# Small products of constants in TensorE's planned idle time, in the first chunks of an attention and two-MLP kernel

## The chip, the core and the metric

The kernel runs on one core of one Trainium2 chip. Its engines each follow an instruction list of their own: TensorE (PE in the profile, with its weight loads as PEld), VectorE (DVE), ScalarE (ACT), GpSimd (POOL, idle here) and SyncE (SP), which issues every DMA. Engines wait for one another through semaphores. The metric is the device time of one execution in microseconds (us), the median over the runs shown.

## The reference

Sparse attention over 4 batches, 8 heads, 576 positions of 64 elements, then two MLPs on the 2304 tokens of width 512 (512 to 2048 to 512, and a gated one, 512 to 1536 to 512). Half of the heads attend to the last 32 positions, the others to every 32nd one.

In short:

```python
scores = scale * np.matmul(q, k.transpose(0, 1, 3, 2))
masks = [mask_local if h < H // 2 else mask_strided for h in range(H)]
attn = softmax(np.where(masks, scores, -1e9))
x = np.matmul(attn, v)
h = x @ w_in;  x = np.maximum(0.01 * h, h) @ w_out
gate = 1.0 / (1.0 + np.exp(-(x @ w_gate)))
out = (gate * (x @ w_val)) @ w_out2
```

## The kernel before

Attention is cut into 8 chunks of 288 tokens (half a batch each), a chunk into groups: a pair of heads each, of up to five blocks of 64 queries (in some chunks a pair is two groups). For every group TensorE makes the scores (`sc`, line 510), VectorE masks and scales them (line 530), takes the row maximum and later normalizes (line 556), ScalarE takes the exponentials (line 541), TensorE transposes the result (`pt`, line 565), ScalarE copies that out (`pts`, line 571), and TensorE multiplies with the values (`xo`, line 582). ScalarE and VectorE then split `xo` into a high and a low half, `x` (lines 601 and 599).

Between the groups TensorE already works on the first MLP, in steps of 256 tokens. A step makes `h` (12 products of 128x128 weights with 256 columns, lines 330 to 332: high by high, high by low, low by high), ScalarE and VectorE apply the activation and split it into `gh` and `gl`, and TensorE makes `y` from these in the same way. Everything in attention is float32; the MLP products are in the rounded form fp32r. VectorE and ScalarE also split the weights, which arrive as 64-bit words (`raw`, `w`, `u`, lines 134 to 187). The second MLP follows after attention and the first one, and is TensorE work almost alone.

The order of the first part is not written out by hand. A planner (`Plan`) holds each step with a cost in ns, what it must come after and which buffers or PSUM banks it takes and gives back. `order` chooses step after step for each engine, notes a start time for each, and the program emits all steps in the order of these starts. Each engine then runs its list strictly in that order and waits where a semaphore isn't there yet, so the planner's times set the order and never the real time. `Plan.order` takes, for a step of TensorE, the later of three times: when the engine comes free, when the data is there, and when the PSUM bank is given back. The constants (`cst`: the 128x128 identity and the masks) come in three DMAs at the start, of which `plan.const[1]` is the identity.

The score banks are `mm0` to `mm3`, which `h` shares; `pt` and `xo` use `ax0` and `ax1`, in the first chunk `xo` takes `ya` and `yb`.

Of the kernel before, what the change touches and what calls it, by code (L numbers as in the profile page):

```python
# [59 lines left out]
RING = 12  # L60
STAGED = 2
EARLY = 2
WORDS = 4
SPLIT = 2
OPS = 12
# [7 lines left out]
def attention_mlp_glu(ctx: ExitStack, tc: tile.TileContext, qT, kl, ks0, ks1, vl, vs0, vs1, w1, w2, wg, wv, w3, const, out):  # L73
    nc = tc.nc
# [13 lines left out]
    def sums_of(i):  # L88
        if i not in sum_y:
            sum_y[i] = res.tile([P, KC, 2 * TP], F32, tag=f"sum{i}", bufs=1, name=f"sum_y{i}")  # L90
        return sum_y[i]

    turn, mm_order = dict.fromkeys(BANKS, 0), [0, 1, 2, 3]

    def bank(tag, shape, name):
        if tag in BANKS:
            n, turn[tag] = turn[tag], (turn[tag] + 1) % BANKS[tag]
            tag = f"{tag}{mm_order[n] if tag == 'mm' else n}"
        return ps.tile(shape, F32, tag=tag, bufs=1, name=name)
# [185 lines left out]
    for c in range(NC2):  # L285
        quarter = {n: parts_tile(("p", c, n), [P, 2, 512]) for n in range(1, 8)}
        for m, w in enumerate((wg, wv)):
            d = {n: quarter[n][:, m, :] for n in quarter}
            a, b = Job((w, 2 * c)), Job((w, 2 * c + 1))
            a.whole = b.whole = False  # L290
            a.dest, b.dest, b.only = [d[1], d[2]], [None, d[3]], 1
            t = Sums(a, b, None, [d[5], d[6]])
# [45 lines left out]
    ident = cst[:, 0:P]  # L338
# [9 lines left out]
    class Plan:  # L348
# [9 lines left out]
        def __init__(self, room):  # L358
            self.ops, self.const, self.late = [], [], []
            self.room = {k: [0.0] * n for k, n in room.items()}  # L360
            self.lanes, self.bus, self.held = [0.0] * 8, 0.0, {}

        def add(self, eng, cost, run, rank, me=None, kind=None, after=(), take=(), give=(), then=()):
            op = {
# [6 lines left out]
        def lend(self, op, name, n):  # L371

            at = len(self.room[name])
            self.room[name] += [None] * n
            self.held[op["n"], name] = [at + i for i in range(n)]
            op["give"] += [(name, op)] * n

        def free(self, after, me, *rooms):

# [2 lines left out]
        def order(self):  # L382

            free = dict.fromkeys(("PE", "DVE", "ACT", "SP", "-"), 0.0)
            last, todo, out = "mm", list(self.ops), []
            held = self.held
            while todo:
                best = None
                for eng in free:
                    can = []  # L390
                    for op in todo:
                        if op["eng"] != eng or any(a["end"] is None for a in op["after"] + op["then"]):
                            continue
                        t = max([0.0 if eng == "-" else free[eng]] + [a["end"] + 40 for a in op["after"]])
                        for k in set(op["take"]):
                            units = sorted(x for x in self.room[k] if x is not None)
                            n = op["take"].count(k)
                            if len(units) < n:
                                t = None
                                break  # L400
                            t = max(t, units[n - 1])
                        if t is None:
                            continue
                        if eng == "PE":
                            t = max(t, free[eng] + self.GAP.get((last, op["kind"]), 0))
                        can.append((t, op))
                    if can:
                        t0 = min(t for t, _ in can) + self.NEAR[eng]
                        t, op = min((c for c in can if c[0] <= t0), key=lambda c: (c[1]["rank"], c[1]["n"]))
                        if best is None or t < best[0]:  # L410
                            best = (t, op)
                assert best, [(o["eng"], o["rank"], o["kind"]) for o in todo[:20]]
                t, op = best
                eng = op["eng"]
                for k in op["take"]:
                    u = min((x, i) for i, x in enumerate(self.room[k]) if x is not None)[1]
                    self.room[k][u] = None
                    op["at"].setdefault(k, []).append(u)
                    held.setdefault((id(op["me"]), k), []).append((op, u))
                    held.setdefault((op["n"], k), []).append(u)  # L420
                if eng == "SP":
                    lane = min(range(8), key=lambda i: self.lanes[i])
                    t = max(t, self.lanes[lane])
                    free[eng] = t + 450
                    self.bus = max(self.bus, t + 1300) + op["cost"] / (280 if t < 25000 else 330)
                    op["end"] = self.lanes[lane] = self.bus + 900
                else:
                    free[eng] = t + op["cost"]
                    op["end"] = t + op["cost"] + self.TAIL[eng]
                    if eng == "PE":  # L430
                        last = op["kind"]
                for k in op["give"]:
                    if isinstance(k, tuple):
                        k, who = k
                        u = held[who["n"], k].pop(0)
                    else:
                        u = held[id(op["me"]), k].pop(0)[1]
                    self.room[k][u] = op["end"] + 40
                todo.remove(op)
                op["start"] = t  # L440
                out.append(op)
            return sorted(out, key=lambda o: o["start"])

    class Group:
# [52 lines left out]
        def scores(self, at):  # L497
            nb, w, cut = self.nb, self.w, self.cut
            sc = [
                bank(f"mm{j + 2 * ('h' in at)}", [P, z - a, w], f"sc{a}") for j, (a, z) in enumerate(((0, cut), (cut, nb)))  # L500
            ]
            for i in range(cut):
                for n in (i, cut + i):
                    if n >= (cut, nb)[n >= cut]:
                        continue
                    q0, k0 = self.q0[n] - self.q0[0], self.k0[n] - self.k0[0]
                    for h in range(2):
                        r = slice(64 * h, 64 * h + 64)
                        o = self.side(n, h)
                        nc.tensor.matmul(  # L510
                            sc[n >= cut][o, n - cut * (n >= cut), :], self.q[r, q0 : q0 + 64], self.k[r, k0 : k0 + w],
                            start=True, stop=True,
                        )
            self.sc = sc
# [45 lines left out]
        def tr(self, a, z, at):  # L560
            if a == 0:
                self.pt = {}
            self.pt[a] = bank(f"ax{at['ax'][0]}", [P, z - a, P], "pt")
            for n in range(a, z):
                nc.tensor.transpose(self.pt[a][: self.w, n - a, :], self.e[:, n, :], ident)  # L565

# [6 lines left out]
        def pv(self, at):  # L573
            nb, w = self.nb, self.w
            total = sum(self.nq)
            self.xo = bank(f"ax{at['ax'][0]}" if "ax" in at else "ya" if "ya" in at else "yb", [P, total], "xo")
            col = 0
            for n in range(nb):
                for h in range(2):
                    r = slice(64 * h, 64 * h + 64)  # L580
                    a = self.side(n, h).start + self.skip[n]
                    nc.tensor.matmul(
                        self.xo[r, col : col + self.nq[n]], self.v[:w, n, r], self.p[:w, n, a : a + self.nq[n]],
                        start=True, stop=True,
                    )
                col += self.nq[n]
# [88 lines left out]
    class First:  # L675
# [11 lines left out]
        def enter(self, last, at):  # L687
            u = unit(self.u[0])
            self.h = bank(f"mm{(at['h'][0] + 2) % 4}", [P, self.T], "h")
            for k in range(KC):  # L690
                xh, xl = xs(self.t0, self.t1, k)
                products(self.h, u, k * P, (k + 1) * P, xh, xl, k == 0, k == KC - 1)
            if last:
                vacant.append(places[self.u[0]])
# [282 lines left out]

    consts = [(P, P + 2 * LW), (0, P), (P + 2 * LW, CONST_W)]

    def load_const(a, z):  # L980
        nc.sync.dma_start(out=cst[:, a:z], in_=const[:, a:z])

    plan = Plan(
        {
            "place": RING, "qk": 3, "v": 2, "e": 3, "st": 3, "sc": 1, "h": 2, "ax": 2, "ya": 1, "yb": 1, "pts": 2, "early": EARLY, "late": EARLY, "raw": STAGED, "w32": WORDS, "split": 1, "late split": SPLIT, "sums": 2,
        }
    )
    unit_done, unit_place = {}, {}
    for j, (a, z) in enumerate(consts):
        op = plan.add("SP", 4 * P * (z - a), lambda at, a=a, z=z: load_const(a, z), rank=((0.5, 1.5, 2.5)[j],), me=plan)  # L990
# [20 lines left out]
    for j in range(RING, RING + n_a):  # L1011
        op = plan.add(
            "SP", 4096 * P, lambda at, j=j: fetch(j), rank=(-2000 + j,), after=[jobs[ready[uses[j]]].kept], then=before,
            take=["place"], me=plan,
# [41 lines left out]
        began = [op]  # L1056
    with tc.manual_schedule(engines={nc.tensor.engine, nc.vector.engine, nc.scalar.engine, nc.sync.engine}):
        for op in plan.order():
            op["run"](op["at"])
    planning.clear()  # L1060
    load_places()
# [96 lines left out]
```

## Time and profile before

| | |
|---|---|
| median of 3 runs | 917.87 us (916.51 to 923.81) |
| profiled execution: its own time | 922.54 us |
| profiled execution: span from the first to the last instruction | 920.7 us |
| TensorE busy | 900.1 us, 98% |
| VectorE busy | 603.7 us, 66% |
| ScalarE busy | 426.7 us, 46% |

The profiled execution lies within the three runs' spread, 4.67 us above their median. In a row of the profile, a line such as L510 is a line of the kernel, an arrow points from what is read to what is written, `128*63 128x128` is the stationary operand and then the output, and x20 counts the records merged into the row. A float32 product leaves two records. Granted clock 1.00 stands for 2.4 GHz and 0.50 for 1.2 GHz. TensorE's matmuls overlap in their records; how fast they follow on one another is read from their starts.

### The profile page before, as it was taken

How to read it: one execution, taken by the hardware profiler on the slowest of the kernel's cores; microseconds unless marked ns; L12 is line 12 of the kernel's file. 1: busy time of each engine (PE TensorE's matmuls, PEld its weight loads, DVE VectorE, ACT ScalarE, POOL GpSimd, SP SyncE). 2: the span in 40 equal slices, each digit the busy share in tenths (PEclk: the TensorE clock that was granted, in tenths of full speed). 3: DMA queues.
4: the chain of work that ended last, by engine and by line, in shares of the span. 5: the costliest groups of instructions: out<-in, count | busy, mean ns of one | idle time of the engine just before them, and what ended most of it. 6: DMA issues, size and time to landing. Idle time of an engine off the chain costs nothing.

```text
span 920.7 us, 16036 instructions
## 1 busy us (share of the span) xinstructions
PE 900.1 (98%) x5904; PEld 818.6 (89%) x5904; DVE 603.7 (66%) x1285; ACT 426.7 (46%) x1127; POOL 0.2 (0%) x4
## 2 busy tenths in 40 slices
PE   6899999999999999999999999999999999999997
PEld 4778888998888999888899999999999999999996
DVE  6798899856877587786796535567535555535554
ACT  6688788644454344443545442243343232243330
POOL 0000000000000000000000000000000000000000
PEclk9889999999999999999999999999999999999999
DMA  8454846767675579664549766555766556755522
GB/s 239 141 153 123 258 127 205 225 217 294 245 241 196 180 264 377 227 206 155 189 134 376 265 209 207 208 210 203 277 214 211 206 207 208 276 208 208 211 79 69
DMA packets 72030, 194.47 MB, mean 211 GB/s; under 512 B 9144, under 2 KB 20760, under 8 KB 71952
## 3 DMA queue, kind: packets, MB, share of 16 engines
q1 hardware_dynamic: 71952, 193.44, 61.2%
q8 instruction: 47, 0.77, 0.3%
q14 instruction: 31, 0.25, 0.1%
HBM read 149.90 MB, written 43.52 MB: 210 GB/s over the span
## 4 chain that ended last, share of the span: by engine, by line
PE 93%; DMA 3%; ACT 2%; DVE 1%; SPq 1%; issue 0%
PE h L330 8%; PE h L331 7%; PE h L332 7%; PE y L330 7%; PE y L331 7%; PE y L332 7%; PE o L934 5%; PE o L933 5%; PE o L932 5%; PE va L889 3%; PE ga L891 3%; PE ga L889 3%; PE ga L890 3%; PE va L890 3%; PE va L891 3%; PE pt L565 2%
## 5 line engine op out<-in xcount | busy, mean ns | idle before, releaser
L330 PE MATMUL h<-x,u 128*128 128x256 f32 (+2 forms) x384 | 133.1, 347 | 0.0
L330 PE MATMUL y<-gh,u 128*128 128x256 f32 (+2 forms) x384 | 131.1, 341 | 0.0
L331 PE MATMUL h<-x,u 128*128 128x256 f32 (+2 forms) x384 | 130.8, 341 | 0.0
L332 PE MATMUL h<-x,u 128*128 128x256 f32 (+2 forms) x384 | 130.7, 340 | 0.0
L331 PE MATMUL y<-gl,u 128*128 128x256 f32 (+2 forms) x384 | 129.3, 337 | 0.0
L332 PE MATMUL y<-gh,u 128*128 128x256 f32 (+2 forms) x384 | 129.3, 337 | 0.0
L937 DVE TENSOR_TENSOR sum_o<-o,sum_o 128x512 f32<-128x512 f32 x90 | 62.1, 691 | 47.2 <-PE o L934 47.2
L704 ACT ACTIVATE gh<-h 128x256 fp32r<-128x256 f32 (+2 forms) x96 | 47.0, 489 | 80.9 <-PE y L332 74.2
L934 PE MATMUL o<-u,gl 128*128 128x512 f32 x216 | 84.4, 391 | 0.0
L933 PE MATMUL o<-u,gh 128*128 128x512 f32 x216 | 84.3, 390 | 0.0
L932 PE MATMUL o<-u,gh 128*128 128x512 f32 x216 | 84.1, 390 | 0.0
L330 PEld LDWEIGHTS h<-x,u 128*128 128x128 f32 x384 | 74.4, 194 | 8.1 <-issue 1.9
L331 PEld LDWEIGHTS h<-x,u 128*128 128x128 f32 x384 | 74.6, 194 | 5.7
L332 PEld LDWEIGHTS h<-x,u 128*128 128x128 f32 x384 | 74.5, 194 | 5.6
L711 DVE TENSOR_TENSOR gl<-g,gh 128x256 fp32r<-128x256 f32 (+2 forms) x96 | 53.3, 555 | 38.9 <-ACT g L707 38.2
L330 PEld LDWEIGHTS y<-gh,u 128*128 128x128 f32 x384 | 72.9, 190 | 6.5 <-issue 0.5
L331 PEld LDWEIGHTS y<-gl,u 128*128 128x128 f32 x384 | 72.9, 190 | 5.7
L332 PEld LDWEIGHTS y<-gh,u 128*128 128x128 f32 x384 | 72.7, 189 | 5.5
L900 ACT COPY k<-ga 128x384 f32<-128x384 f32 x36 | 17.2, 479 | 112.1 <-PE ga L891 112.1
L138 ACT ACTIVATE w<-raw 128x512 f32<-128x512 f32 x68 | 45.8, 674 | 39.8 <-DMA raw<-w 22.6
L541 ACT ACTIVATE e<-e,st 128x96 f32<-128x96 f32 (+2 forms) x160 | 58.0, 369 | 9.1 <-DVE st L536 9.0
L918 DVE TENSOR_TENSOR gl<-gate,gh 128x384 fp32r<-128x384 f32 x72 | 40.0, 556 | 26.3 <-ACT gh L917 24.3
(105 smaller groups left out, 1886.0 us busy)
## 6 DMA issues: line engine op xcount, KB each, us to landing
u<-parts SPq DMA_DIRECT2D x182, 512.0 KB
raw<-w SPq DMA_DIRECT2D x44, 512.0 KB
parts<-split SPq DMA_DIRECT2D x84, 256.0 KB
parts<-split SPq DMA_DIRECT2D x32, 512.0 KB
raw<-wg SPq DMA_DIRECT2D x12, 512.0 KB
raw<-wv SPq DMA_DIRECT2D x12, 512.0 KB
out<-sum_o SPq DMA_DIRECT2D x16, 256.0 KB
v<-vl SPq DMA_DIRECT2D x14, 240.0 KB
```

The costliest lines, as they stand in the source:

```text
L330: nc.tensor.matmul(o, wu[:, 0, a:b], xh, start=start, stop=False)
L331: nc.tensor.matmul(o, wu[:, 0, a:b], xl, start=False, stop=False)
L332: nc.tensor.matmul(o, wu[:, 1, a:b], xh, start=False, stop=stop)
L541: nc.scalar.activation(out=e[:, n, :], in_=e[:, n, :], func=AF.Exp, bias=st[:, 0, n : n + 1], scale=1.0, accum_out=st[:, 1, n : n + 1],)
L711: nc.vector.tensor_tensor(out=gl, in0=self.c, in1=gh.bitcast(F32), op=ALU.subtract)
L889: nc.tensor.matmul(o, wh, xh, start=first and k == 0, stop=False, **more)
L890: nc.tensor.matmul(o, wh, xl, start=False, stop=False, **more)
L891: nc.tensor.matmul(o, wl, xh, start=False, stop=k == 1, **more)
L932: nc.tensor.matmul(o, gh[:, r], u[:, 0, :], start=f == 0, stop=False)
L933: nc.tensor.matmul(o, gh[:, r], u[:, 1, :], start=False, stop=False)
L934: nc.tensor.matmul(o, gl[:, r], u[:, 0, :], start=False, stop=f == 1)
L937: nc.vector.tensor_tensor(out=acc, in0=o, in1=acc, op=ALU.add)
```

## The change

`order` now notes for each TensorE step that takes a bank how long the planner has the engine idle before it with the bank already free: the planned start less the later of the engine's and the bank's own time. When the step is emitted, 100 ns are taken off that time and the rest is divided by 150 ns. That many products of the identity with itself (128x128 stationary, up to 128 columns and mostly 64) are emitted ahead of the step, into the bank that the step overwrites anyway. Only steps that the planner starts before 60 us get any, and only where the idle time begins after the planned landing of the identity. Nothing reads what these products write.

```diff
+WARM_SPARE, WARM_SLOT, WARM_END = 100, 150, 60000
...
+    warm = [0]
...
-            self.lanes, self.bus, self.held = [0.0] * 8, 0.0, {}
+            self.lanes, self.bus, self.held, self.times = [0.0] * 8, 0.0, {}, {}
...
+        def room_time(self, k, u):
+            return self.times[k, u]
...
                 for k in op["take"]:
-                    u = min((x, i) for i, x in enumerate(self.room[k]) if x is not None)[1]
+                    free_at, u = min((x, i) for i, x in enumerate(self.room[k]) if x is not None)
                     self.room[k][u] = None
+                    self.times[k, u] = free_at
...
+                if eng == "PE" and op["take"]:
+                    op["idle"] = t - max([free[eng]] + [self.room_time(k, u) for k in op["at"] for u in op["at"][k]])
...
             ]
+            keep_warm(sc[0][:, 0, :])
             for i in range(cut):
...
+            keep_warm(self.pt[a][:, 0, 0:64])
             for n in range(a, z):
...
+            keep_warm(self.xo[:, 0:64])
             col = 0
...
+            keep_warm(self.h[:, 0:64])
             for k in range(KC):
...
+    def keep_warm(o):
+        for _ in range(warm[0]):
+            nc.tensor.matmul(o, ident, ident[:, : o.shape[-1]], start=True, stop=True)
+        warm[0] = 0
...
         for op in plan.order():
+            if op["eng"] == "PE":
+                idle = op.get("idle", 0) - WARM_SPARE
+                warm[0] = int(max(0, idle) / WARM_SLOT) if plan.const[1]["end"] < op["start"] - idle < WARM_END else 0
             op["run"](op["at"])
```

Ten steps get such products, 54 in all: 4 and 3 ahead of the scores of the third and fourth group, 8 ahead of the first `pt`, 11 and 4 ahead of the second and the fourth `xo`, 1 ahead of the scores of the fifth group, 5 ahead of the first `h` (these 36 before the first chunk's MLP work), then 6 ahead of the second chunk's first `pt`, and 6 and 6 ahead of a `pt` and an `xo` of its strided heads. Beyond these rows the lists of all five engines hold the same instructions in the same order as before (line numbers apart).

TensorE's list in the first chunk, from the end of the fourth group's scores on, before (`first_qk` and `first_v` are the first chunk's queries, keys and values):

```order
L510 MATMUL sc_228<-first_qk 64x63 x2
L565 MATMUL pt<-cst,e 96x128 x8
L582 MATMUL xo<-pts,first_v 64x64 x8
L582 MATMUL xo<-pts,first_v 64x32 x2
L565 MATMUL pt<-cst,e 96x128 x2
L565 MATMUL pt<-cst,e 63x128 x3
L582 MATMUL xo<-pts,first_v 64x64 x8
L582 MATMUL xo<-pts,first_v 64x32 x2
```

And the same place now:

```order
L519 MATMUL sc_232<-first_qk 64x63 x2
L994 MATMUL pt<-cst 128x64 x8
L575 MATMUL pt<-cst,e 96x128 x8
L593 MATMUL xo<-pts,first_v 64x64 x8
L593 MATMUL xo<-pts,first_v 64x32 x2
L575 MATMUL pt<-cst,e 96x128 x2
L575 MATMUL pt<-cst,e 63x128 x3
L994 MATMUL xo<-cst 128x64 x11
L593 MATMUL xo<-pts,first_v 64x64 x8
L593 MATMUL xo<-pts,first_v 64x32 x2
```

The rows of line 994 are new: 8 products ahead of the first transposes and 11 ahead of the second group's `xo`; neither of the two bursts has a semaphore of its own to wait for, so each begins as soon as the row above it is done.

TensorE's list where the second chunk's first scores end and the first chunk's `y` begins, before:

```order
L510 MATMUL sc_510<-k,q 64x63 x2
L565 MATMUL pt<-cst,e 96x128 x5
L330 MATMUL y<-gh,u_506 128x256
L331 MATMUL y<-gl,u_506 128x256
L332 MATMUL y<-gh,u_506 128x256
```

And now:

```order
L519 MATMUL sc_546<-k,q 64x63 x2
L994 MATMUL pt<-cst 128x64 x6
L575 MATMUL pt<-cst,e 96x128 x5
L332 MATMUL y<-gh,u_542 128x256
L333 MATMUL y<-gl,u_542 128x256
L334 MATMUL y<-gh,u_542 128x256
```

Six products stand between the scores and the transposes; the `y` products follow as they did.

## Rows read from the trace of the kernel before

**Rows 1.** The page, busy time of TensorE over the span: us, share, instructions.

```profile
PE 900.1 (98%) x5904; PEld 818.6 (89%) x5904; DVE 603.7 (66%) x1285; ACT 426.7 (46%) x1127; POOL 0.2 (0%) x4
```

**Rows 2.** Span and mean granted TensorE clock of the core (share of full speed).

```profile
core 0: 920.7 us, clock 0.990
```

**Rows 3.** Busy time by engine in stretches of 5 us, one of 80: us, records, granted clock, DMA.

```profile
20.00:25.00 5.00, 4.86 (x66) 4.12 (x65) 4.14 (x12) 3.30 (x9) 0.00 (x0) 1.00 0.70 174
25.00:30.00 5.00, 5.00 (x42) 4.84 (x41) 3.18 (x7) 2.88 (x14) 0.00 (x0) 1.00 0.23 64
30.00:35.00 5.00, 2.48 (x35) 2.06 (x29) 4.79 (x16) 3.27 (x14) 0.00 (x0) 0.77 0.57 144
35.00:40.00 5.00, 5.00 (x55) 4.22 (x55) 1.95 (x7) 3.01 (x15) 0.00 (x0) 0.55 0.26 91
...
50.00:55.00 5.00, 4.81 (x43) 4.14 (x44) 4.97 (x18) 4.88 (x25) 0.00 (x0) 0.50 0.72 229
55.00:60.00 5.00, 5.00 (x67) 4.47 (x66) 3.70 (x13) 3.92 (x18) 0.00 (x0) 0.84 0.28 82
...
95.00:100.00 5.00, 4.19 (x42) 3.60 (x42) 2.87 (x12) 2.04 (x8) 0.00 (x0) 0.75 0.86 286
120.00:200.00 80.00, 79.06 (x869) 73.14 (x870) 65.98 (x192) 55.17 (x205) 0.00 (x0) 1.00 0.58 186
```

**Rows 4.** TensorE in order of time: start, us, line, what, idle before and releaser.

```profile
9.72 0.90 PE L510 MATMUL sc<-first_qk 64*64 64x63 f32 x20 [1.62 <-DMA first_qk<-ks]
10.55 1.30 PE L565 MATMUL pt<-cst,e 128*96 128x128 f32 x5
...
16.30 0.91 PE L582 MATMUL xo<-pts,first_v 96*64 96x64 f32 x12
17.74 0.64 PE L582 MATMUL xo<-pts,first_v 96*64 96x64 f32 x8 [0.53 <-ACT pts L571]
...
21.58 1.29 PE L582 MATMUL xo<-pts,first_v 63*64 63x63 f32 x20
23.01 1.23 PE L510 MATMUL sc<-k,q 64*64 64x96 f32 x20
24.16 0.58 PE L330 MATMUL h<-x,u 128*128 128x256 f32 x1
...
25.18 0.41 PE L331 MATMUL h<-x,u 128*128 128x256 f32 x1
25.39 0.41 PE L332 MATMUL h<-x,u 128*128 128x256 f32 x1
```

**Rows 5.** The same view of TensorE, further on, up to 60 us.

```profile
33.48 1.28 PE L565 MATMUL pt<-cst,e 128*96 128x128 f32 x5 [1.22 <-DVE e L556]
...
37.24 1.28 PE L582 MATMUL xo<-pts,v 96*64 96x64 f32 x20
...
42.02 0.78 PE L582 MATMUL xo<-pts,v 96*64 96x64 f32 x20
...
43.24 0.28 PE L332 MATMUL y<-gh,u 128*128 128x256 f32 x1
43.36 0.29 PE L330 MATMUL y<-gh,u 128*128 128x256 f32 x1
...
47.02 0.54 PE L565 MATMUL pt<-cst,e 128*63 128x128 f32 x3 [1.24 <-DVE e L556]
```

**Rows 6.** The chain that ended last, in order of time, first 100 us: start, us, what.

```profile
12.42 10.45 DMA k<-kl
```

**Rows 7.** ScalarE in order of time, first 24 us.

```profile
11.66 0.72 ACT L571 COPY pts<-pt 96x384 f32<-96x384 f32 x2
14.40 0.66 ACT L138 ACTIVATE w<-raw 128x512 f32<-128x512 f32 x1 [2.02 <-DMA raw<-w]
```

**Rows 8.** VectorE in order of time, 24 to 60 us.

```profile
30.21 0.26 DVE L530 SCALAR_TENSOR_TENSOR e<-sc,cst 128x96 f32<-128x96 f32 x1 [1.37 <-PE sc L510]
...
39.96 0.36 DVE L530 SCALAR_TENSOR_TENSOR e<-sc,cst 128x189 f32<-128x189 f32 x1 [2.38 <-PE sc L510]
```

## The prediction

> **What bounds the kernel now.** I read the shares first: TensorE is busy for 900.1 of 920.7 us [rows 1, 2], so nearly all of the time is TensorE's own, and a change can only shorten its work, speed its clock or close the 20.6 us of gaps. Next the granted clock: its mean is 0.990 [rows 2], which over 920.7 us is 9.2 us of full speed not given. The table by stretches shows where: 0.77 and 0.55 between 30 and 40 us, 0.50 and 0.84 between 50 and 60, 0.75 between 95 and 100, and 1.00 elsewhere [rows 3]. At half speed for the missing part, these are (0.23 + 0.45) x 5 / 0.5 = 6.8 us, then 6.6 us, then 2.5 us at 1.2 GHz.
>
> The first 30 us read 1.00 too, but the reader shouldn't believe it. Two `h` products of 256 columns start 0.21 us apart at 25.18 and 25.39 us; two `y` products of the same size start 0.12 us apart at 43.24 and 43.36 us [rows 4, 5]. 256 columns in 0.21 us are 1.2 GHz. So the engine runs at the low level from the start until the `h` products of the first chunk, although it is busy for 4.86 of 5 us between 20 and 25 [rows 3].
>
> What does the low clock cost? Before 23 us little: the scores at 23.01 us need keys that are under way until 22.87 us, the chain runs through this DMA [rows 6, 4], and no faster TensorE gets past it. From 24.16 us on TensorE is itself what ends last: VectorE waits for its scores for 1.37 us at 30.21 and for 2.38 us at 39.96 us [rows 8]. Later the work is without slack (79.06 of 80 us busy from 120 to 200 us [rows 3]), so what is gained before 60 us reaches the end.
>
> **The change: what it adds.** 54 products and nothing else; no wait of another engine is new. No row has a full-width float32 product of 64 columns, so its price is bounded. An `xo` step has 20 records for 10 products of half the array's width, in pairs side by side, and takes 1.28 us at the low clock and 0.78 us at the high one [rows 5]: 0.128 us and 0.078 us each. One that fills the width can't lie beside another, so twice that, less the tail at the end of the step: 0.21 us low, 0.12 us high. These are the spacings of the `h` and `y` products too [rows 4, 5]. Below stands 0.064 us, the spacing of the records; above 0.43 us, if the two weight loads of each product hide behind nothing. I take 0.21 and 0.12: 54 x 0.21 = 11.3 us, or 6.5 us at the high clock. All of it is TensorE work; what is left to see is how much falls into gaps.
>
> **Where the added work lies.** The 4 and 3 products ahead of the scores go into gaps: the fourth scores wait 1.62 us for their DMA [rows 4], against 3 x 0.21 = 0.6 us. The 8 ahead of the first `pt` don't. The planner must have had at least 8 x 0.15 + 0.1 = 1.3 us idle there, but in the trace the fourth scores came late (9.72 to 10.62 us) and `pt` follows at 10.55 us with no gap [rows 4]: 8 x 0.21 = 1.7 us go onto TensorE's path. Part is taken back, because ScalarE's copies of `pt` at 11.66 us are followed by 2.02 us of waiting for weights until 14.40 us [rows 7]. The 11 ahead of the second `xo` are 2.3 us at 16.3 us, against a gap of 0.53 us at 17.74 us [rows 4]; 4, 1 and 5 follow, 0.9, 0.3 and 1.1 us, with hardly a gap. By hand through the rows, at the low clock all along, `xo` of the fourth group moves from 21.58 to some 24.1 us, and the first `h` from 24.16 to some 27.8 us: 3.6 us late. If the clock rises in or behind the eleven, at 19 to 22 us, all behind them halves, the late keys bind again at 22.9 us, and `h` begins at 24.6 to 25.2 us: I charge **+0.7 us**.
>
> **What the clock gives back.** First, 24 `h` products at 0.12 in place of 0.21 us: 2.2 us less, of which VectorE, with work of its own in hand, lets through about the 1.37 us that it waits [rows 8]: **-1.4 us**. Second, from 33.48 to 39.5 us: `pt` 1.28 us and `xo` 1.28 against 0.78 us [rows 5], so 0.5 us for each, 12 `y` products 12 x 0.09 = 1.1 us, the small steps behind them 0.5 us: **-2.6 us**; VectorE's 2.38 us of waiting [rows 8] and what it gains ahead of that let this through. It needs the clock to hold across the gaps after `h`; of these the six products (0.7 us) fill about half of the 1.22 us at 33.48 us [rows 5]. Third, from 50 to 56.6 us: 12 `h` products 1.1 us and 0.6 us of `pt` and `xo`, but VectorE and ScalarE are busy for 4.97 and 4.88 of 5 us up to 55 us [rows 3], so **-1.2 us**. The last twelve products cost nothing here: a `pt` waits 1.24 us for VectorE at 47.02 us [rows 5] where 6 x 0.12 = 0.7 us go in, and it is these gaps after which the clock falls. The stretch at 95 to 100 us lies behind the last product, so nothing. Sum: 0.7 - 1.4 - 2.6 - 1.2 = -4.5 us, from 922.54 to 918.0 us.
>
> **Does it raise the clock at all?** Up to 24 us the engine works on `pt`, `xo` and scores with few gaps, and stays at 1.2 GHz until the dense `h` products [rows 3, 4]: being busy isn't enough, the kind of work counts. At the end of the stretch from 35 to 40 us the clock rose behind `y`, `xo` and `pt` [rows 3, 5]; bursts of products over the full width should do. The Trainium skill, TensorE: Matmul & The Clock Gate, section Part 4: PE-mode transpose, says that a transpose does not count as busy for the clock in the way an ordinary product does. The trace agrees as far as it goes: 4.86 of 5 us busy, much of it transposes, raised nothing. By that rule the added products, being ordinary ones, are just what was missing, and the sum stands; if all busy time counted alike, they would add nothing that the engine lacked, and the sum would be that of the second rival.
>
> **From the profiled execution to the median.** The median is 4.67 us below the execution that I sum from. I take the spread (916.51 to 923.81) for executions in which such slow stretches fall more or less often: the two before 60 us cost up to 3.4 and 3.3 us each. Then the change takes from the median run less than 4.5 us, and more than nothing: I take 2.4, a bit over half. **917.87 - 2.4 = 915.5 us.**
>
> **Rivals.** *The added products run into the path and the clock doesn't rise for them in time* (slower than before). The place is TensorE's list from 10.55 to 24.16 us, the mechanism that the planner's gaps aren't there in the trace, the price 3.6 us: 921.5 us. It decides from a price of 0.2 us a product, if the clock isn't up by some 22 us. For it: no gap at 10.55 us [rows 4]. Against it: the eleven products and their neighbours are dense. With 0.43 us a product the 29 from the eight to the five alone are 12.5 us, of which the late keys and small waits hide about 2.5: 10 us more, 927.9 us.
>
> *The clock moves and nothing comes of it*, or it doesn't move and the products lie in gaps: VectorE and ScalarE at 4.97 and 4.88 of 5 us [rows 3] take over what TensorE gives, or the clock falls again in the gaps after `h`. 917.9 us, within 1.5 us. For it: 6 of the 54 products stand in the gaps after `h`, and `pt` waits for VectorE there and at 47.02 us [rows 5]. Against it: VectorE's own waits for TensorE at 30.21 and 39.96 us [rows 8] are longer than what it would have to make up.
>
> *All of it is removed, and the median run had as much to remove*: -1.4 - 2.6 - 1.7 with the full third term, and the stretch at 95 us gone by luck (2.5 to 3.4 us at half speed, 1.7): -7.4 us, 910.5 us.
>
> **How the numbers follow.** My forecast 0.48, the delayed path 0.20 (and 0.04 for the dear product), no effect 0.21, all removed 0.07. The range goes from 911 to 921.5 us: it leaves out the dear product, half of the last rival and the tails of the others. About 1%, 9.2 us, is what a measurement of this kernel can tell from no change. All clock loss on record is 9.2 us, so faster by over 1% needs it whole: 0.04. Slower by over 1% is the dear product: 0.04. Within 1%: 0.92.
>
> **What would show it.** Right, if in the profile after: the `h` products at 24 to 28 us start 0.12 us apart; the stretches from 30 to 40 and from 50 to 60 us read 1.00; the mean clock is nearer to 0.997; the first `h` starts before 25.3 us; the added products are 0.21 us apart at first and 0.12 later; and everything past 120 us is the same, only earlier. Wrong, if `h` starts past 26 us, if the clock falls at 33 us as before, or if VectorE's and ScalarE's waits between 40 and 55 us grow by what TensorE gains. The forecast of the median would be wrong, with the mechanism right, if the runs' spread has nothing to do with the clock.

## The result and the profile after

The median is 929.39 us over 6 runs (926.40 to 930.66), that of the kernel before on the same chips 916.40 us. The ratio is 1.0126, with a 95% interval of 1.0088 to 1.0164: slower by 1.3%, where 915.5 us within 911 to 921.5 was forecast. The profiled execution took 927.33 us.

The page of the changed kernel, its span and TensorE's busy time, records and weight loads (as [rows 1]):

```profile
span 925.6 us, 16251 instructions
...
PE 911.2 (98%) x6012; PEld 832.2 (90%) x6012; DVE 603.3 (65%) x1285; ACT 426.2 (46%) x1127; POOL 0.2 (0%) x4
```

TensorE is busy for 11 us more than before, 911.2 against 900.1 us [rows 1], with 108 more records: 54 products, two records each. Its mean granted clock is 0.999, against 0.990 [rows 2]. So from 40 us on the clock no longer falls, as was meant, and the time still grew. The stretches of 5 us (one of 80) that answer to [rows 3]:

```profile
20.00:25.00 5.00, 5.00 (x33) 4.88 (x34) 2.16 (x7) 1.10 (x3) 0.00 (x0) 1.00 0.56 144
25.00:30.00 5.00, 5.00 (x49) 4.54 (x45) 2.69 (x8) 3.42 (x10) 0.00 (x0) 1.00 0.02 5
30.00:35.00 5.00, 5.00 (x52) 4.42 (x52) 2.89 (x9) 1.29 (x4) 0.00 (x0) 1.00 0.10 22
35.00:40.00 5.00, 5.00 (x27) 5.00 (x27) 2.21 (x5) 1.57 (x8) 0.00 (x0) 1.00 0.12 39
...
50.00:55.00 5.00, 4.79 (x83) 4.34 (x83) 5.00 (x18) 4.40 (x22) 0.00 (x0) 1.00 0.94 313
55.00:60.00 5.00, 4.88 (x87) 4.28 (x87) 4.65 (x14) 5.00 (x24) 0.00 (x0) 1.00 0.89 282
...
95.00:100.00 5.00, 5.00 (x76) 4.43 (x77) 4.16 (x17) 3.97 (x18) 0.00 (x0) 1.00 0.70 201
120.00:200.00 80.00, 79.42 (x901) 73.16 (x900) 70.75 (x209) 57.62 (x215) 0.00 (x0) 1.00 0.55 175
```

From 30 to 60 us and at 95 us the clock now reads 1.00, where it read 0.77, 0.55, 0.50, 0.84 and 0.75 before; up to 39 us that is not its real level, as the starts below show. TensorE has no gap from 20 to 40 us, while VectorE and ScalarE (third and fourth figure) are busy for 1.1 to 3.4 us of 5. TensorE in order of time shows with what it is busy (rows that answer to [rows 4, 5] among them):

```profile
6.63 1.97 PE L994 MATMUL sc<-cst 128*128 128x63 f32 x8
...
11.67 3.67 PE L994 MATMUL pt<-cst 128*128 128x64 f32 x16
...
19.66 4.79 PE L994 MATMUL xo<-cst 128*128 128x64 f32 x22
...
33.33 2.39 PE L994 MATMUL h<-cst 128*128 128x64 f32 x10
35.49 0.56 PE L332 MATMUL h<-x,u 128*128 128x256 f32 x1
...
36.06 0.41 PE L334 MATMUL h<-x,u 128*128 128x256 f32 x1
36.27 0.41 PE L332 MATMUL h<-x,u 128*128 128x256 f32 x1
...
39.43 0.28 PE L332 MATMUL h<-x,u 128*128 128x256 f32 x1
39.55 0.28 PE L333 MATMUL h<-x,u 128*128 128x256 f32 x1
...
42.97 1.55 PE L994 MATMUL pt<-cst 128*128 128x64 f32 x12
```

Line 994 are the added products. The eleven ahead of the second `xo` take 22 records and 4.79 us, where the prediction had 2.3 us; one record follows another after (4.79 - 0.42) / 21 = 0.208 us on average, where 0.42 us is the length of the last one. The eight ahead of the first `pt` take 3.67 us, not 1.7 us. The first `h` starts at 35.49 us instead of 24.16 us [rows 4], 11.33 us late. And it still starts at the low level: two `h` products are 0.21 us apart at 36.06 us. They are 0.12 us apart only from 39.43 us on, behind 3.8 us of `h` itself. The clock did not rise for any of the 36 products ahead of it; in the kernel before, too, it rose only within these `h` products, at 29.2 us. Later, at the high clock, twelve records take 1.55 us, 0.116 us apart: a product costs 0.23 us there, where 0.12 was forecast.

The view of line 994 has the durations of the records, least, median and most in ns:

```profile
L994 PEld LDWEIGHTS xo<-cst x42: 188/333/338, 19.4 to 58.3; 128*128 128x128 f32 x42
L994 PE MATMUL xo<-cst x42: 222/421/421, 19.7 to 58.3; 128*128 128x64 f32 x42
```

A weight load of the identity lasts 333 ns at the low clock (30 of the 42 ran at it), the product 421 ns, and there is one load for each record. The chain that ended last (start, us, what) runs through the bursts themselves:

```profile
11.74 3.60 PE pt L994 x16
...
19.87 4.59 PE xo L994 x22
```

How the 11.33 us travel through the program is read from the starts of the `h` products in both traces, the kernel before and the change:

| `h` product | before, us | after, us | late by, us |
|---|---|---|---|
| 1st | 24.16 | 35.49 | 11.33 |
| 25th | 52.73 | 60.92 | 8.19 |
| 37th | 57.88 | 64.38 | 6.50 |
| 121st | 97.05 | 103.38 | 6.33 |
| 133rd | 104.38 | 109.24 | 4.86 |
| 1141st | 497.11 | 501.93 | 4.82 |

The held clock gives back 4.83 us by the 37th product. Another 1.5 us come behind 97 us, where the kernel before had the stretch at 0.75 [rows 3]. No added product lies there, and a second trace of the kernel before (the first experiment) reads 1.00 from 95 to 105 us, so this part is the luck of one execution. From there to the end the lateness stays between 4.8 and 5.4 us. The two spans differ by 4.9 us, as the table does, and the medians by 13.0 us. The profiled execution of the kernel before was one with more low clock than most, as the first experiment shows, and what it lost there a typical execution has not to lose. The change has such executions of its own: three of its six read a mean clock of 0.996 and took 929.99 to 930.66 us.

### The profile page after: what moved, and what is told of

It is laid out like the page before. It is cut to its first block, busy times and chain, and to the rows that moved or that the text cites. A ratio compares the mean times of both kernels' runs of the same rounds, so it can differ in the third digit from the quotient of the medians.

```text
span 925.6 us, 16251 instructions
## 1 busy us (share of the span) xinstructions
PE 911.2 (98%) x6012; PEld 832.2 (90%) x6012; DVE 603.3 (65%) x1285; ACT 426.2 (46%) x1127; POOL 0.2 (0%) x4
## 4 chain that ended last, share of the span: by engine, by line
PE 93%; ACT 2%; DVE 2%; DMA 2%; SPq 0%; issue 0%
PE h L332 7%; PE h L333 7%; PE h L334 7%; PE y L332 7%; PE y L333 7%; PE y L334 7%; PE o L945 5%; PE o L946 5%; PE o L944 5%; PE va L901 3%; PE ga L903 3%; PE ga L901 3%; PE ga L902 3%; PE va L903 3%; PE va L902 3%; PE xo L593 2%
## 5 line engine op out<-in xcount | busy, mean ns | idle before, releaser
L332 PEld LDWEIGHTS h<-x,u 128*128 128x128 f32 x384 | 73.3, 191 | 7.9 <-issue 1.7
L333 PEld LDWEIGHTS h<-x,u 128*128 128x128 f32 x384 | 73.3, 191 | 5.6
L334 PEld LDWEIGHTS h<-x,u 128*128 128x128 f32 x384 | 73.3, 191 | 5.7
```

What stands on the lines that cost most here:

```text
L332: nc.tensor.matmul(o, wu[:, 0, a:b], xh, start=start, stop=False)
L333: nc.tensor.matmul(o, wu[:, 0, a:b], xl, start=False, stop=False)
L334: nc.tensor.matmul(o, wu[:, 1, a:b], xh, start=False, stop=stop)
```

## The experiments

Theory A: a product costs two weight loads of about 0.21 us at the low clock, whatever its columns; the 36 ahead of the first `h` lie on TensorE's path and do not raise the clock, and that is the whole loss. Rivals: the later 18 cost it; the columns set the price; something else of the change costs it (banks, waits); products of constants cannot raise the clock at all. Each run is compared with the kernel before on the same chip, and is an edit of the changed kernel where nothing else is said. Each version has one trace.

**The kernel before once more.** No edit.

> The kernel before, unchanged. Theory A (the profiled execution was one with more low clock than most): its executions show mean granted clocks between 0.990 and 0.997, the span grows as the clock falls, about 0.9 us for each 0.001, and most lie near 915 to 918 us. Rival (the spread has another cause): times between 914 and 924 us with clocks that do not go with them.

918.19 us median over 12 executions, ratio 1.0011 (0.9993 to 1.0029). Time goes with the clock, loosely: the three executions with a mean granted clock of 0.998 took 915.44 to 915.97 us, the three at 0.990 to 0.992 took 919.14 to 923.26 us; in between there is less order (0.997: 916.54 to 919.51). Of the 78 executions of the kernel before that stand beside these experiments, the 26 at 0.998 have a median of 915.97 us and the 11 at 0.992 one of 918.96 us: 3 us for 0.006, a little over half of what was expected. So the low clock in the middle of the program comes and goes, and the execution from which the prediction was summed (0.990, 922.54 us) was among those with the most of it. The medians here, 916.40 and 918.19 us, lie 4 to 6 us below it; so much less has a typical execution to gain.

**Only the 36 products ahead of the first `h`.**

```diff
+    bursts = [0]
...
+        if warm[0]:
+            bursts[0] += 1
-        for _ in range(warm[0]):
+        for _ in range(warm[0] if bursts[0] <= 7 else 0):
```

> Only the 36 products ahead of the first chunk's MLP work. Theory A (they cost two records of 0.21 us each at the low clock, on TensorE's path, and raise nothing): the first h product starts near 35.5 us as with all 54, 11 us late, and the time is 929 to 933 us. Rival (the later 18 are the costly ones, through the work they delay): h still late in the trace, but the time is back at 916 to 921 us.

928.75 us, ratio 1.0104 (1.0062 to 1.0147): the whole loss is in these. TensorE in order of time, and one row of the stretches of 5 us:

```profile
19.66 4.79 PE L998 MATMUL xo<-cst 128*128 128x64 f32 x22
...
35.48 0.56 PE L332 MATMUL h<-x,u 128*128 128x256 f32 x1
```

```profile
45.00:50.00 5.00, 5.00 (x39) 4.67 (x38) 3.06 (x10) 3.35 (x18) 0.00 (x0) 0.50 0.45 144
```

`h` starts at 35.48 us, as with all 54. Without the later 18 the clock falls again (0.50 from 45 to 50 us), and in this trace the 37th `h` product is 4.5 us later than with them (68.87 against 64.38 us). One of the four executions took 918.88 us, the others 928.27 to 930.98; it has no trace, so what it did differently isn't known.

**Only the 18 behind it** (`bursts[0] > 7` in the same place).

> Only the 18 products behind the first chunk's h. Theory A: nothing is late at 24 us, the products run at the high clock in gaps at about 0.23 us each, the low clock between 50 and 57 us is gone in most executions; 913 to 917 us, ratio 0.995 to 1.001. Rival (each product costs its time wherever it is): 18 x 0.23 = 4 us more, 920 us.

914.74 us, ratio 0.9978 (0.9964 to 0.9992): the later 18 gain 0.2%. TensorE in order of time:

```profile
32.27 2.44 PE L998 MATMUL pt<-cst 128*128 128x64 f32 x12
34.50 1.27 PE L575 MATMUL pt<-cst,e 128*96 128x128 f32 x5
...
53.53 0.28 PE L334 MATMUL h<-x,u 128*128 128x256 f32 x1
53.65 0.28 PE L332 MATMUL h<-x,u 128*128 128x256 f32 x1
```

And the kernel before, at the same products:

```profile
53.31 0.41 PE L332 MATMUL h<-x,u 128*128 128x256 f32 x1
53.52 0.41 PE L330 MATMUL h<-x,u 128*128 128x256 f32 x1
```

Two things are in these rows. At 53 us the `h` products are 0.12 us apart, where they were 0.21 us before. But the six at 32.27 us did not hold the clock in this trace: their twelve records take 2.44 us, so the low level is back, and `pt` starts at 34.50 instead of 33.48 us [rows 5]. In the trace of the change the same six, at 42.97 us, took 1.55 us, and the clock held.

**The price, by columns and by weights.** Half the columns (32 moving), with all 54:

```diff
-            nc.tensor.matmul(o, ident, ident[:, : o.shape[-1]], start=True, stop=True)
+            nc.tensor.matmul(o[:, :32], ident, ident[:, :32], start=True, stop=True)
```

> All 54 products, with 32 columns in place of 64 (63 and 96). If the price is that of the two weight loads, a record still takes 0.2 us at the low clock, h starts near 35 us and the time stays at 928 to 931 us. If it is that of the columns, a record takes 0.11 us, h starts near 30 us and the time is 921 to 924 us.

928.61 us, ratio 1.0126 (1.0106 to 1.0147), the same as the change:

```profile
19.55 4.74 PE L994 MATMUL xo<-cst 128*128 128x32 f32 x22
...
35.16 0.56 PE L332 MATMUL h<-x,u 128*128 128x256 f32 x1
```

The 22 records take 4.74 us against 4.79: half the columns cost as much as all 64. Now a quarter of the weights (32 of the 128 columns of the identity) with the 64 columns moving:

```diff
-            nc.tensor.matmul(o, ident, ident[:, : o.shape[-1]], start=True, stop=True)
+            nc.tensor.matmul(o[:32], ident[:, 0:32], ident[:, : o.shape[-1]], start=True, stop=True)
```

> All 54 products with 32 columns of the identity as weights in place of 128, 64 columns moving. If the price was that of loading 128 columns: the load falls to a quarter, the 64 columns bind with 0.107 us a record, half of the change's 0.208; h starts near 29 us, 919 to 923 us. If the load costs the same whatever its width: h near 35 us, 927 to 931 us.

914.79 us, ratio 0.9976 (0.9960 to 0.9991), 4 us below the range expected and faster than the kernel before:

```profile
6.63 1.05 PE L994 MATMUL sc<-cst 128*32 128x63 f32 x8
...
14.45 0.78 PE L593 MATMUL xo<-pts,first_v 96*64 96x64 f32 x20
...
16.15 1.42 PE L994 MATMUL xo<-cst 128*32 128x64 f32 x22
...
23.59 0.39 PE L332 MATMUL h<-x,u 128*128 128x256 f32 x1
...
30.68 0.94 PE L575 MATMUL pt<-cst,e 128*96 128x128 f32 x5 [0.43 <-DVE e L565]
31.27 0.56 PE L332 MATMUL y<-gh,u 128*128 128x256 f32 x1
```

The first burst takes 1.05 us for 8 records, against 1.97 us for the same burst of the change. Its records start 0.105 us apart, 0.21 us a product: that is the price the prediction had assumed. The `xo` at 14.45 us takes 0.78 us, as at the high clock [rows 5], so the clock is up ahead of the eleven, where in the change it rose at 39.4 us; the eleven at 16.15 us take 1.42 us for 22 records. The first `h` starts at 23.59 us, 0.6 us earlier than in the kernel before. That is no gain shown: the run of fourteen products below has none ahead of `h` and starts it at 22.56 us, so this start moves by more than that between executions. The clock still falls behind it: the first `y` product at 31.27 us lasts 0.56 us, like one at the low level.

**The kind of work and the clock.** The 54 in fp32r, with one record each (GpSimd copies the identity into an fp32r tile first):

```diff
+    twice = x1[:, 0, 0, 0 : 2 * P]
...
+        if a == 0:
+            for n in range(2):
+                nc.gpsimd.tensor_copy(twice[:, n * P : (n + 1) * P], ident)
...
-            nc.tensor.matmul(o, ident, ident[:, : o.shape[-1]], start=True, stop=True)
+            nc.tensor.matmul(o[:, : o.shape[-1] // 2 * 2], twice[:, 0:P], twice[:, : o.shape[-1] // 2 * 2], start=True, stop=True)
```

> The same 54 products in the rounded form fp32r (the identity copied into an fp32r tile by GpSimd; widths 62, 64 and 96). One record each in place of two. If the price is one weight load a record: 0.21 us a product at the low clock (0.11 if the load of this form is shorter), h starts near 28 us (or 26), and the time is 919 to 922 us if the clock stays low up to there; if this form raises the clock early, h products start 0.12 us apart and it is 914 to 917 us.

919.47 us, ratio 1.0042 (1.0025 to 1.0059). Then two such products for each of the 54, with up to 256 columns (`keep_warm` is given the whole bank for it):

```diff
...
-        for _ in range(warm[0]):
-            nc.tensor.matmul(o, ident, ident[:, : o.shape[-1]], start=True, stop=True)
+        w = min(256, o.shape[-1] // 2 * 2)
+        for _ in range(2 * warm[0]):
+            nc.tensor.matmul(o[:, :w], twice[:, 0:P], twice[:, :w], start=True, stop=True)
```

> Each product replaced by two fp32r products of up to 256 columns, like those of h: 0.21 us a record at the low clock, so the same time on TensorE as the change, but with columns streaming all of it. If it was the kind of work (weight loads for half the time or more) that kept the clock low, it rises during the eleven or the four, by some 25 us, h starts near 30 us and runs at 0.12 us a product: 919 to 924 us. If products of constants do not raise it in any form, h starts at 35 us at the low clock: 927 to 931 us.

918.09 us, ratio 1.0015 (1.0006 to 1.0024), 1 us below the range expected. TensorE in order of time, the 64 columns and then the 256:

```profile
16.54 2.54 PE L995 MATMUL xo<-x 128*128 128x64 f32 x11
...
27.84 0.56 PE L332 MATMUL h<-x,u 128*128 128x256 f32 x1
```

```profile
12.18 2.82 PE L996 MATMUL pt<-x 128*128 128x256 f32 x16
14.84 0.71 PE L576 MATMUL pt<-cst,e 128*96 128x128 f32 x5
...
17.68 2.87 PE L996 MATMUL xo<-x 128*128 128x256 f32 x22
...
26.98 0.28 PE L332 MATMUL h<-x,u 128*128 128x256 f32 x1
```

The eleven products of 64 columns take 2.54 us for 11 records: a weight load in this form takes 0.21 us too, and one record costs as much as one with 256 columns. Behind them the clock is still low (the first `h` product at 27.84 us lasts 0.56 us). With 256 columns the 16 records at 12.18 us take 2.82 us, less than 16 x 0.21 = 3.4 us; the five `pt` products behind them take 0.71 us, as at the high clock, against 1.30 us before [rows 4]; and the 22 at 17.68 us take 2.87 us. So products of the identity can raise the clock, in fp32r here and in float32 with narrow weights above: in the three traces with these two forms (the third is the last experiment) it is up by 14 us, in the nine others it rose between 27 and 40 us, within the `h` products. Zeros in the data or the number format aren't what kept it low in the change. The forms differ in more than one way, and no run separates which difference it is.

**Placed by the trace's gaps** (an edit of the kernel before). Fourteen full-width float32 products: none ahead of `h`, 4 ahead of the seventh scores (written into the bank of the next `pt`, taken early), 4 ahead of that `pt`, 3 and 3 in the second chunk's last group.

```diff
+            if op is sc7:
+                pt["me"].early_pt = bank(f"ax{pt['at']['ax'][0]}", [P, 3, P], "pt")
+                keep_warm(pt["me"].early_pt[:, 0, 0:64], 4)
+            if op is pt:
+                keep_warm(pt["me"].early_pt[:, 0, 0:64], 4)
...
+            if self is groups[7]:
+                keep_warm(self.xo[:, 0:64], 3)
```

> 14 products only, placed by the trace's gaps and not by the planner's: 4 ahead of the seventh scores (into the bank of the next pt), 4 ahead of that pt, 3 and 3 ahead of a pt and the xo of the second chunk's last group. Theory A: each runs at the high clock (0.23 us) inside its gap, the clock holds through 33 us and through 50 us in most executions, the y products at 34 us start 0.12 us apart; 911 to 914 us, ratio 0.993 to 0.997. Rival (the gaps at 30 to 33 us are too long even so): the clock falls at 33 us, and the time is that of the 18, 914 to 916 us.

915.46 us, ratio 0.9976 (0.9961 to 0.9991):

```profile
22.56 0.58 PE L330 MATMUL h<-x,u 128*128 128x256 f32 x1
...
28.21 1.10 PE L985 MATMUL pt<-cst 128*128 128x64 f32 x8
...
30.30 1.10 PE L985 MATMUL pt<-cst 128*128 128x64 f32 x8
31.59 0.72 PE L566 MATMUL pt<-cst,e 128*96 128x128 f32 x5 [0.18 <-DVE e L557]
...
32.38 0.28 PE L332 MATMUL y<-gh,u 128*128 128x256 f32 x1
32.50 0.28 PE L330 MATMUL y<-gh,u 128*128 128x256 f32 x1
```

Of the two gaps, [rows 5] has the second (1.22 us); the first, in the kernel before:

```profile
31.17 0.33 PE L510 MATMUL sc<-k,q 64*64 64x63 f32 x4 [1.01 <-PE sc L510]
```

Each burst of four takes 1.10 us in the gaps that were 1.01 and 1.22 us, the clock holds, and `y` runs 0.12 us apart at 32.4 us, as theory A has it. But the median is over the 911 to 914 us expected and in the range of the rival: the clock held, and that was worth less than theory A had.

**The change with the price corrected** (the planner's 150 ns set to 450): 15 products, 9 of them ahead of the first `h`.

> The change with 450 in place of 150 ns as the planner's price, near the 420 ns that a product takes at the low clock: 15 products in place of 54, 9 of them ahead of the first h. If the price alone made the loss: 9 x 0.42 = 3.8 us, of which the gaps ahead of the scores and the late keys hide most; the first h starts at 24 to 26 us, 915 to 919 us. If something else of the change costs (the banks taken early, the waits in TensorE's list), h still starts 5 us late or more and the time is over 921 us.

917.50 us, ratio 1.0003 (0.9990 to 1.0016):

```profile
16.03 1.38 PE L994 MATMUL xo<-cst 128*128 128x64 f32 x6
...
24.63 0.56 PE L332 MATMUL h<-x,u 128*128 128x256 f32 x1
```

`h` starts at 24.63 us, 0.5 us after that of the kernel before. One number in the planner takes the loss away, and what else the change does (banks taken early, waits in TensorE's list) costs nothing that these runs can tell.

**Narrow weights and real gaps together.** The narrow products, 4 in place of 8 ahead of the first `pt`, 8 and 9 in the two gaps behind `h`.

> Products with 32 columns of weights, as in the run with narrow loads, with 4 in place of 8 ahead of the first pt, and 8 more ahead of the seventh scores and 9 in place of 6 ahead of the next pt, so that both gaps behind h are filled. If the two gains add: the clock is up by some 16 us, h products are 0.12 us apart, the clock holds at 30 to 34 us; 911.5 to 913.5 us, ratio 0.994 to 0.997. If what h gains is waited off at VectorE and ScalarE by 45 us: 914 to 915.5 us, like either alone.

914.78 us, ratio 0.9975 (0.9959 to 0.9991):

```profile
27.07 1.08 PE L995 MATMUL pt<-cst 128*32 128x64 f32 x16
...
29.16 1.19 PE L995 MATMUL pt<-cst 128*32 128x64 f32 x18
...
30.93 0.36 PE L332 MATMUL y<-gh,u 128*128 128x256 f32 x1
```

The clock holds from 15 us on in this trace (`y` at 30.93 us lasts 0.36 us), and its 47.08 us for the 25th `h` is 5.7 us ahead of the kernel before (52.73 us). But the median is that of either alone: the gains do not add over the executions. With this, the narrow products, the 18 and the fourteen are four versions that are faster than both kernels, by 0.2 to 0.25% of the kernel before and none told apart from the others. That is little: the kernel before, measured against itself in the first experiment, came out 0.1% apart.

## Why the prediction was wrong

- **What bounds the kernel, and where the clock is low.** Right: after and before differ in TensorE's busy time and clock, and the shift at 104 us is the one at the end (4.86 and 4.82 us), within 0.6 us on the way.
- **The price of a product.** This is the step that failed. I took 0.21 us at the low clock and 0.12 us at the high one, from the spacing of `xo`, doubled, and put down 0.43 us as the upper bound "if the two weight loads of each product hide behind nothing". Measured: 2 x 0.208 = 0.42 us and 2 x 0.116 = 0.23 us. The doubled `xo` was the wrong row: its weights are 64 columns wide, and a product of the identity loads 128, twice. The 32-column run, where the columns halved and the time didn't, and the run with narrow weights, where the price came out as I had it, show that it is the load and not the columns.
- **Where the added work lies.** The place was right, TensorE's list from 10.5 us on, where the planner's gaps aren't there; the size followed the price: 11.33 us late, where I had 3.6 us without the clock and 0.7 us with it, so most of the difference is the price. My rival of the dear product, 10 us more and 927.9 us, is what happened; I gave it 0.04. That its time lies 1.5 us from the median is in part luck: it had 10 us where the trace shows 11.33 and the medians 13.0.
- **The clock rises in or behind the eleven.** Wrong for the products of the change: it rose at 39.4 us, within `h`. With narrow weights, and with the dense ones, it was up ahead of the eleven already (14.45 and 14.84 us). The condition on which I charged 0.7 us instead of 3.6 was not met. My reading of the trace was wrong, too: of the 4.86 us busy between 20 and 25 us, transposes are 0.69 us (two, at 20.96 us), and the rest is `xo`, scores and `h`. Of the page cited ahead of the result (the Trainium skill, TensorE: Matmul & The Clock Gate, Part 4: PE-mode transpose) this stretch is therefore hardly a test. By that rule, as I drew on it, the added products, being ordinary ones, were to raise the clock; that was not enough, as 4.79 us of them back to back show.
- **What the clock gives back.** Of the first term (-1.4 us at `h`) 0.5 us came, since 18 of the 24 products ran at the low level. The second and third (-2.6 and -1.2 us) came as -4.3 us between the 24th and the 37th `h`, a little more than forecast. The 1.5 us behind 97 us were not forecast and, as said, are luck.
- **That the later products cost nothing.** Right in the sum: alone they gain 0.2%. But in that trace six of them ran mostly at the low clock and moved a `pt` by 1 us.
- **From the execution to the median.** The reading of the spread was right in direction: time goes with the clock, if loosely. And the 2.4 us that I took from a typical execution were about what there was: the last experiment, with the clock up from 15 us on, is 2.3 us below the kernel before (914.78 against 917.09 us). This also means that the gain sized on the profiled execution is mostly absent in a typical one, while the loss is in all six executions of the change (926.40 us and more): 929.39 - 916.40 = 13.0 us in the medians, 4.9 us in the two traces.

The Trainium skill, TensorE: Matmul & The Clock Gate, LDWEIGHTS (loading the stationary operand), puts a weight load at the number of columns over 1.2 in ns; by that, an estimate for 128 columns is 107 ns. At the high clock the runs are near it: records bound by such a load stand 0.116 us apart. At the low clock they don't agree: 0.208 us in float32, and 2.54 us for eleven in fp32r. The measurement decides.

Not settled: why the gains of the narrow products and of the filled gaps don't add in the median, what the one fast execution of the 36 did, why the clock stayed low behind the wide products and not behind the others, and what still lowers it in some executions of nearly every version (down to 0.995 in the last one).

## What to carry to other kernels

The products put in here to keep TensorE's clock up were paid in weight loads, and the same number with 32 weight columns in place of 128 cost no time. So price such a product by the row of one with the same weights, or time it in a trace, before a planner fills gaps with it. A planner's gap is no gap until the trace shows it; work put into one that isn't there lay on the path in all six executions of the change, while the low clock that it was to prevent was there only in some. When executions of one kernel spread, look at the granted clock of each before summing gains from one of them.

## What the hardware showed that was not expected

- 4.79 us of back-to-back full-width float32 products, and all seven bursts ahead of `h` (16.9 us within 29 us), left TensorE at 1.2 GHz; behind 16 fp32r products of 256 columns, or behind narrow float32 ones, it was at 2.4 GHz at 14.84 and 14.45 us.
- A product of 32 columns costs what one of 64 costs (4.74 against 4.79 us for 22 records) with 128 columns of weights; with 32 columns of weights it costs about half at the low clock (1.05 against 1.97 us for 8).
- The granted clock reads 1.00 from the start of every trace, while the work up to the first rise (29.2 us in the kernel before, 39.4 us in the change) is spaced as at 1.2 GHz: `h` products 0.21 us apart. The mean granted clock leaves this part out.
